# Two more chunks transposed by DMA, a last tile in two halves, and another order of the first slots

## The chip, the cores and the metric

The kernel runs on one NeuronCore of a Trainium2 chip. The metric is the device time of one execution in microseconds (us). The program uses five engines: TensorE (PE in the profile, with its weight loads as PEld), VectorE (DVE), ScalarE (ACT), GpSimd (POOL) and SyncE (SP). Loads that convert float32 to bfloat16 are issued by POOL; stores and DMA transposes are issued by SP. All transfers run on the same 16 DMA engines.

## The reference

The reference has two stages. The first is a retention layer over 4 batches, 8 heads, 768 positions and 64 dimensions per head; the second is a feed-forward layer on its output, with a "snake" activation. Cut to what is computed:

```python
gamma = 1.0 - 2.0 ** (-5.0 - np.arange(H))          # one decay per head
for t in range(S):
    state = gamma[None, :, None, None] * state + np.einsum('bhd,bhe->bhde', k[:, :, t], v[:, :, t])
    y[:, :, t] = scale * np.einsum('bhd,bhde->bhe', q[:, :, t], state)
x = y.transpose(0, 2, 1, 3).reshape(B * S, H * D)   # 3072 tokens x 512
h = x @ w_in                                        # 512 -> 2048
s = np.sin(alpha * h)
g = h + s * s / (alpha + 1e-09)
out = g @ w_out                                     # 2048 -> 512
```

## The kernel before, in words

The positions of a batch are cut into six chunks of 128, so there are 24 chunks. The list `order` (also called `P`) holds them in the order of their processing: first the opening chunk of each of the four batches (P[0] to P[3], named e0 to e3), then the rest of each batch. Counted from one, the seventh and eighth chunks are P[6] and P[7]; below they are called P6, P7 and so on. The chunks form groups of 4, 2, 4, 4, 4, 4 and 2 token tiles (`sizes`), and the feed-forward layer works on one group at a time.

A chunk goes through these steps:

- `load_chunk` (L83) brings q, k and v from HBM into bfloat16 tiles, three transfers issued on POOL's queue. `scale_v` (L112) multiplies v by decay factors, on DVE or POOL.
- q and k must be transposed. `stage_T` (L190 to L200) does it with eight TensorE transposes into a PSUM bank and one copy to the tile qkT on DVE or ACT. `turn` (L202 to L205) does it with one DMA transpose from SBUF to SBUF on SP's queue. The tile qkT has six buffers. Before the change, the chunks up to P7 use TensorE, and P8 and later ones use `turn`.
- `stage_A` (L207 to L218) multiplies k by q for each head (eight matmuls into the PSUM tile pa) and DVE multiplies by a mask (tile aT, L217).
- `stage_M` (L236 to L260) multiplies by v and by the running state, and writes the chunk's columns of xT, the feed-forward layer's input. `stage_S` and `keep_S` (L220 to L234) carry the state.

The feed-forward layer is written as `Slot`s. A Slot is one block of 128 hidden features (or two, with nf=2): four matmuls per block into the PSUM tile ph (L279), a sine on ACT (L282), a square on ACT or DVE (`sq`, L287 or L289), and on DVE the addition that gives gT (`add`, L294). The second matmul of the layer is `ff_out` (L304): 16 matmuls accumulate a 128x512 token tile in the PSUM tile po, then ACT copies it to o_sb (L316) and SP stores it (L317). The very last tile is copied in two halves, by DVE (L313) and then ACT (L314), and stored by one transfer.

PSUM has eight banks, which the program divides as four buffers with the tag mm, two banks with the tag pa, one with ty and one with ps. A buffer is taken again when its last reader has finished.

The order of the work is written out by hand, engine by engine; each engine runs its own list in order and waits for the others by semaphores. The order has these stretches: a start with e0 to e2; "early" Slots 0 to 7 over the first three tiles of group 0, with e3 worked in between; Slots 8 to 15 with the first pieces of `ff_out` for group 0 (helper `F`) and with P4 and P5 worked in; then `phase(1, ...)`, which runs group 1's Slots (nf=2) with the rest of group 0's output. A table in the call of phase 1 says behind which Slot the steps of P6 to P11 stand: T for `stage_T`, X for `turn`, A for `stage_A`, M for `stage_M`. The phases of groups 2 to 6 follow, and the last group's output tiles end the kernel.

Of the kernel before, what the change touches and what calls it, by code (L numbers as in the profile page):

```python
# [8 lines left out]
F32 = mybir.dt.float32  # L9
# [6 lines left out]
def kernel(  # L16
# [15 lines left out]
    nc = tc.nc  # L32
    B, H, S, D = q.shape
    C = 128
# [3 lines left out]
    d_model = H * D  # L38
    d_ff = moe_w_in.shape[1]
    KS = d_model // 128  # L40
    FF = d_ff // 128
# [7 lines left out]
    sizes = [4, 2, 4, 4, 4, 4, 2]  # L49
    assert sum(sizes) == NJ  # L50
    NG = len(sizes)
    groups = [order[sum(sizes[:g]):sum(sizes[:g + 1])] for g in range(NG)]
# [4 lines left out]
    work = ctx.enter_context(tc.tile_pool(name="work", bufs=2))  # L57
    psum = ctx.enter_context(tc.tile_pool(name="psum", bufs=1, space=bass.MemoryType.PSUM))
# [5 lines left out]
    w_out = big.tile([128, FF, d_model], BF16, name="w_out")  # L64
# [4 lines left out]
    def chunk_of(t, j):  # L69
        b, c = divmod(j, NCH)  # L70
        return t[b, :, c * C:(c + 1) * C, :].rearrange("h s d -> s h d")

    def load_chunk(j, names="qkv"):
        for name, src in (("q", q), ("k", k), ("v", v)):
            if name not in names:
                continue
            if name == "v":
                t = big.tile([128, H, D], BF16, name="vr", tag="vr", bufs=NJ)
            else:
                if ("qk", j) not in raw:  # L80
                    raw["qk", j] = big.tile([128, 2, H, D], BF16, name="qkr", tag="qkr", bufs=NJ)
                t = raw["qk", j][:, "qk".index(name)]
            nc.gpsimd.dma_start(out=t, in_=chunk_of(src, j))  # L83
            raw[name, j] = t
# [105 lines left out]
    def stage_T(j, eng=None, tag="ty"):  # L190
        pt = psum.tile([128, 2 * NP, 128], BF16, name="pt", tag=tag, bufs=4 if tag == "mm" else 1)
        st["qkT", j] = work.tile([128, 2 * NP, 128], BF16, name="qkT", tag="qkT", bufs=6)
        for i in range(2):
            for p in range(NP):
                nc.tensor.transpose(pt[:, i * NP + p, :],  # L195
                                    raw["qk"[i], j][:, 2 * p:2 * p + 2, :].rearrange("p h d -> p (h d)"), ident)
        if eng is nc.scalar:
            nc.scalar.copy(st["qkT", j], pt)
        else:
            nc.vector.tensor_copy(st["qkT", j], pt)  # L200

    def turn(j):  # L202

        st["qkT", j] = work.tile([128, 2 * NP, 128], BF16, name="qkT", tag="qkT", bufs=6)
        nc.sync.dma_start_transpose(out=st["qkT", j], in_=raw["qk", j].rearrange("p i h d -> p (i h d)"))  # L205

    def stage_A(j):  # L207
        qkT = st["qkT", j]
        pa = psum.tile([128, 2, NP, 128], F32, name="pa", tag="pa")
        for p in range(NP):  # L210
            for e in range(2):
                r = slice(64 * e, 64 * e + 64)
                nc.tensor.matmul(pa[:, e, p, :], qkT[r, NP + p, :], qkT[r, p, :],  # L213
                                 start=(p == 0), stop=True, skip_group_check=True)
        aT = work.tile([128, 2, NP, 128], BF16, name="aT", tag="aT", bufs=2)
        m = dec.rearrange("p e n t -> p (e n) t") if j % NCH == 0 else mask_bc
        nc.vector.tensor_mul(aT.rearrange("p e n t -> p (e n) t"), pa.rearrange("p e n t -> p (e n) t"), m)  # L217
        st["aT", j] = aT  # L218
# [17 lines left out]
    def stage_M(j):  # L236
        c = j % NCH
        g, i = place[j]
        if g not in xT:
            xT[g] = work.tile([128, KS, sizes[g] * C], BF16, name="xT", tag="xT", bufs=3)  # L240
        qkT, aT, vs = st["qkT", j], st["aT", j], raw["v", j]
        py = psum.tile([128, NP, 128], F32, name="py", tag="ty")
        if c > 0:
            for p in range(NP):
                for e in range(2):
                    r = slice(64 * e, 64 * e + 64)
                    nc.tensor.matmul(py[r, p, :], s_bd[c % 2][:, p, r], qkT[:, p, :],  # L247
                                     start=(p == 0), stop=True, skip_group_check=True)
        for p in range(NP):
            for e in range(2):  # L250
                nc.tensor.matmul(py[64 * e:64 * e + 64, p, :], vs[:, 2 * p + e, :], aT[:, e, p, :],  # L251
                                 start=(c == 0 and p == 0), stop=True, skip_group_check=True)
        x = xT[g][:, :, i * C:(i + 1) * C]
        if c == 0:
            nc.scalar.copy(x, py)
            return
        ps = stage_S(j) if c < NCH - 1 else None
        nc.vector.tensor_mul(x, py, qg[:, c])  # L258
        if ps is not None:
            keep_S(j, ps)  # L260


    gT = {}
# [32 lines left out]

    out_view = out.rearrange("(t p) n -> p t n", p=128)
    po = {}
    end = (NG - 1, sizes[-1] - 1)

    def ff_out(g, ts, f):
        if (g, ts) not in po:
            po[g, ts] = psum.tile([128, d_model], F32, name="po", tag="mm", bufs=4)
        nc.tensor.matmul(po[g, ts], gT[g][:, f, ts * C:(ts + 1) * C], w_out[:, f, :],  # L304
                         start=(f == 0), stop=(f == FF - 1))
        if f == FF - 1:
            take(g, ts)

    def take(g, ts):
        o_sb = work.tile([128, d_model], F32, name="o_sb", tag="o_sb", bufs=3)  # L310
        if (g, ts) == end:
            h = d_model // 2
            nc.vector.tensor_copy(o_sb[:, :h], po[g, ts][:, :h])  # L313
            nc.scalar.copy(o_sb[:, h:], po[g, ts][:, h:])  # L314
        else:
            nc.scalar.copy(o_sb, po[g, ts])  # L316
        nc.sync.dma_start(out=out_view[:, groups[g][ts], :], in_=o_sb)  # L317

    def out_pieces(g, tss):
        return [lambda ts=ts, f=f: ff_out(g, ts, f) for ts in tss for f in range(FF)]  # L320
# [13 lines left out]
    e0, e1, e2, e3 = order[:B]  # L334
# [40 lines left out]
    def phase(g, outs, att, nf=1):  # L375

        no, done = len(outs), 0
        for n in range(FF // nf):
            now = Slot(g, n * nf, nf=nf).sq("A")
            for fn in att.get(n, ()):  # L380
                fn()
            now.add()
            while done < no * (n + 1) * nf // FF:
                outs[done]()
                done += 1

    def T(j):
        return lambda: stage_T(j)

    def X(j):  # L390
        return lambda: turn(j)

    def A(j):
        return lambda: stage_A(j)

    def M(j):
        return lambda: stage_M(j)

    def SK(j):
        return lambda: keep_S(j, stage_S(j))  # L400
# [3 lines left out]
    P = order  # L404
    n3, n4 = 3 * C, 4 * C
    def F(ts, fs):
        for f in fs:
            for t in ts:
                ff_out(0, t, f)

    def early(f, tag="mm"):
        return Slot(0, f, (0, n3), tag=tag)

    a = early(0)
    decay_table(3)
    scale_v(e0, nc.vector)
    for t in s_bd:
        nc.vector.memset(t, 0.0)
    b = early(1)
    a.sq("A").add()  # L420
    a = early(2)
    b.sq("A")
    c = early(3)
    a.sq("A")
    stage_T(e3)
    b.add()
    b = early(4, "ps")
    c.sq("A")
    a.add()
    a = early(5)  # L430
    b.sq("A")
    stage_A(e3)
    c.add()
    c = early(6)
    a.sq("A")
    b.add()
    b = early(7)
    c.sq("A")
# [9 lines left out]
    a = Slot(0, 0, (n3, n4), 4)  # L448
    F((1,), (3,))
    a.sq("A").add()  # L450
    a = Slot(0, 8)
    b = Slot(0, 4, (n3, n4), 4)
    a.sq("A").add()
    a = Slot(0, 9)
    b.sq("D").add()
    F((0, 1), (4,))
    b = Slot(0, 10)
    a.sq("A").add()
    F((0, 1), (5,))
    a = Slot(0, 11)  # L460
# [3 lines left out]
    b = Slot(0, 12)  # L464
# [3 lines left out]
    a = Slot(0, 13)  # L468
    b.sq("D").add()
    F((0, 1), (9,))  # L470
    b = Slot(0, 14)
    a.sq("A").add()
    F((0, 1), (10,))
    stage_T(P[4], nc.scalar, "mm")
    a = Slot(0, 15)
    b.sq("D").add()
    a.sq("A").add()
    F((0, 1), (11, 12))
    stage_A(P[4])
    scale_v(P[4], nc.vector)  # L480
    F((0, 1), (13, 14))
    stage_T(P[5], nc.scalar, "mm")
    F((0, 1), (15,))


    load_chunk(P[7])
    load_chunk(P[8])
    scale_v(P[6], nc.gpsimd)
    load_chunk(P[9])
# [13 lines left out]
    def fill(n):  # L503
        for _ in range(n):
# [9 lines left out]
    stage_M(P[5])  # L514
    fill(4)
    phase(1, outs,
          {0: [T(P[6]), X(P[8])], 1: [A(P[6])], 2: [T(P[7]), X(P[9])], 3: [A(P[7]), M(P[6])], 4: [X(P[10])],
           5: [A(P[8]), M(P[7])], 6: [X(P[11]), A(P[9]), M(P[8]), SK(e1)], 7: [M(P[9])]}, 2)
    for g in range(2, NG):
        att = {}  # L520
        if g + 1 < NG:
            js = groups[g + 1]
            for i, j in enumerate(js):
                a = i * FF // len(js) + 1
                n = P.index(j) + 2
# [6 lines left out]
                    att[a].append(SK(j - 1))  # L532
            att.setdefault(FF - 2, []).append(M(js[-1]))
        phase(g, out_pieces(g - 1, range(sizes[g - 1])), att, 1 if sizes[g] > 2 else 2)
    for fn in out_pieces(NG - 1, range(sizes[-1])):
        fn()
# [1 line left out]
_INS = ['q', 'k', 'v', 'moe_w_in', 'moe_w_out', 'moe_alpha']  # L538
_OUTS = [((3072, 512), 'float32')]
# [25 lines left out]
```

## Time and profile before

The median of nine runs is 219.32 us (218.60 to 220.13). The profiled execution took 220.1 us.

| what | value |
|---|---|
| profiled execution, its own time | 220.1 us |
| its span in the profile | 218.3 us |
| PE busy | 208.0 us (95%) |
| ACT busy | 162.7 us (75%) |
| DVE busy | 128.3 us (59%) |
| POOL busy | 90.0 us (41%) |
| granted TensorE clock | 1.00 |
| DMA transposes (L205), landing after issue | 16, median 5.6 us, 3.1 to 8.6 |
| TensorE transposes of whole chunks (L195) | 40 |
| stores of out tiles, landing after issue | 24, median 2.3 us |

The span runs from the program's first instruction to its last; the time of an execution also holds what lies around it. In the profile a line such as `L279` is a line of the kernel; `out<-in` names the tile written and the tile read. In the timeline a bracket at the end of a row tells how long the engine stood idle before it and what ended that idle time. SPq and POOLq are the instructions with which SP and POOL start transfers.

### The profile page before, as it was taken

Reading aid. Unit: us, or ns where it says so; the run is one execution under the profiler, and the core shown is the slowest. Engines: PE = TensorE matmul, PEld = TensorE weight load, DVE = VectorE, ACT = ScalarE, POOL = GpSimd, SP = SyncE. Lnnn points to the kernel's source line nnn. Section 1 sums busy time; section 2 is a strip of 40 time slices with the busy share of each in tenths; the row PEclk is TensorE's granted clock in tenths of the full one; section 3 lists DMA queues with packets and bytes.
Section 4 is the critical chain, followed back from the end, with each engine's and each line's share of the span. In section 5 each row is a group of like instructions: output and inputs, shape, how many; then the busy total and the mean of one; then the engine's idle time right before and its main releaser. Section 6 shows DMA issues by size and latency. Waiting matters only on the chain.

```text
span 218.3 us, 4245 instructions
## 1 busy us (share of the span) xinstructions
PE 208.0 (95%) x1661; PEld 107.9 (49%) x1661; DVE 128.3 (59%) x213; ACT 162.7 (75%) x311; POOL 90.0 (41%) x105
## 2 busy tenths in 40 slices
PE   7998898999999999999999999999999999999992
PEld 3544553457764544445455445455444544555540
DVE  4686669776896767766466556476464555233310
ACT  7678796558888899798778768768878876766620
POOL 8975333999689797796982000000000000000000
PEclk9999999999999999999999999999999999999999
DMA  9999999999999999999999146136011101111121
GB/s 132 152 192 191 206 207 163 140 196 162 138 146 197 139 162 161 104 147 156 154 193 125 24 96 85 34 77 95 6 50 51 48 0 51 48 48 48 51 92 52
DMA packets 99508, 24.67 MB, mean 113 GB/s; under 512 B 92304, under 2 KB 96416, under 8 KB 99488
## 3 DMA queue, kind: packets, MB, share of 16 engines
q0 software_dynamic: 77024, 13.37, 82.7%
q1 hardware_dynamic: 22464, 11.02, 26.2%
q8 instruction: 13, 0.21, 0.4%
q14 instruction: 7, 0.06, 0.1%
HBM read 27.27 MB, written 6.29 MB: 154 GB/s over the span
## 4 chain that ended last, share of the span: by engine, by line
PE 74%; DMA 12%; POOL 4%; DVE 4%; ACT 2%; issue 1%; POOLq 0%
PE po L304 35%; PE ph L279 30%; DMA qkr<-in_k_dram 8%; DMA w_in<-in_moe_w_in_dram 4%; PE py L247 3%; PE pa L213 2%; POOL qkr L83 2%; PE py L251 2%; DVE aT L217 1%; POOL vr L83 1%; DVE xT L258 1%; PE ps L227 1%; DVE gT L294 1%; PE pt L195 1%; ACT s L282 1%
## 5 line engine op out<-in xcount | busy, mean ns | idle before, releaser
L294 DVE SCALAR_TENSOR_TENSOR gT<-s,rec_alpha,ph 128x512 bf16<-128x512 f32 (+3 forms) x120 | 74.2, 638 | 68.9 <-ACT s L287 68.3
L304 PE MATMUL po<-w_out,gT 128*128 128x512 bf16 x384 | 98.5, 380 | 0.6 <-DVE gT L294 0.6
L279 PE MATMUL ph<-xT,w_in 128*128 128x512 bf16 (+3 forms) x480 | 98.0, 336 | 0.6 <-DVE gT L294 0.2
L282 ACT ACTIVATE s<-ph,alpha_sb 128x512 f32<-128x512 f32 (+3 forms) x120 | 69.7, 602 | 33.7 <-PE ph L279 33.5
L279 PEld LDWEIGHTS <-w_in 128*128 128x128 bf16 x480 | 45.5, 98 | 42.0 <-issue 1.5
L287 ACT ACTIVATE s<-s 128x512 f32<-128x512 f32 (+1 forms) x94 | 58.4, 621 | 2.6
L304 PEld LDWEIGHTS <-gT 128*128 128x128 bf16 x384 | 35.2, 98 | 38.2 <-issue 0.6
L112 POOL TENSOR_TENSOR vr<-vr,kg 128x512 bf16<-128x512 bf16 x21 | 22.1, 1066 | 12.7 <-DMA vr<-in_v_dram 12.7
L217 DVE TENSOR_TENSOR aT<-pa,mask 128x1024 bf16<-128x1024 f32 x20 | 24.4, 1221 | 0.2 <-PE pa L213 0.2
L83 POOL DMA_DIRECT2D vr<-in_v_dram x24 | 21.8, 910 | 3.2 <-DMA w_in<-in_moe_w_in_dram 1.7
L83 POOL DMA_DIRECT2D qkr<-in_q_dram x23 | 21.3, 927 | 3.7 <-DMA w_out<-in_moe_w_out_dram 1.7
L83 POOL DMA_DIRECT2D qkr<-in_k_dram x23 | 20.6, 895 | 5.3 <-DMA w_out<-in_moe_w_out_dram 4.9
L234 ACT CAST s_bd<-ps 64x256 bf16<-64x256 f32 x40 | 14.4, 360 | 2.4 <-PE ps L227 2.1
L316 ACT COPY o_sb<-po 128x512 f32<-128x512 f32 x23 | 13.1, 576 | 3.9 <-PE po L304 3.9
L258 DVE TENSOR_TENSOR xT<-py,qg 128x512 bf16<-128x512 f32 x20 | 13.7, 685 | 2.5 <-PE py L251 2.4
L328 PE MATMUL spare<-warm 128*128 128x512 bf16 x28 | 10.2, 488 | 1.2 <-DVE warm L131 1.2
L213 PEld LDWEIGHTS <-qkT 64*128 64x128 bf16 x192 | 5.4, 94 | 9.3 <-issue 6.9
L251 PE MATMUL py<-aT,vr 128*64 128x128 bf16 x192 | 9.5, 220 | 0.4 <-DVE rec_alpha L366 0.2
L213 PE MATMUL pa<-qkT 64*128 64x128 bf16 x192 | 9.5, 219 | 0.2
L247 PE MATMUL py<-qkT,s_bd 128*64 128x128 bf16 x160 | 8.3, 224 | 0.7 <-DVE xT L258 0.6
L247 PEld LDWEIGHTS <-s_bd 128*64 128x64 bf16 x160 | 5.4, 109 | 4.7 <-issue 2.0
L251 PEld LDWEIGHTS <-vr 128*64 128x64 bf16 x192 | 6.9, 110 | 1.3 <-issue 1.0
(59 smaller groups left out, 69.8 us busy)
## 6 DMA issues: line engine op xcount, KB each, us to landing
out_dram<-o_sb SPq DMA_DIRECT2D x24, 256.0 KB, 2.3
vr<-in_v_dram POOLq DMA_DIRECT2D x24, 128.0 KB, 5.9
qkr<-in_q_dram POOLq DMA_DIRECT2D x23, 128.0 KB, 5.6
qkr<-in_k_dram POOLq DMA_DIRECT2D x23, 128.0 KB, 5.9
w_in<-in_moe_w_in_dram POOLq DMA_DIRECT2D x4, 512.0 KB, 11.1
w_out<-in_moe_w_out_dram POOLq DMA_DIRECT2D x4, 512.0 KB, 14.8
q<-in_q_dram SPq DMA_DIRECT2D x1, 256.0 KB, 3.2
k<-in_k_dram SPq DMA_DIRECT2D x1, 256.0 KB, 4.0
```

Source lines behind the costliest of these rows:

```text
L83: nc.gpsimd.dma_start(out=t, in_=chunk_of(src, j))
L112: eng.tensor_mul(raw["v", j], raw["v", j], kg[:, j % NCH, :, None].to_broadcast([128, H, D]))
L213: nc.tensor.matmul(pa[:, e, p, :], qkT[r, NP + p, :], qkT[r, p, :], start=(p == 0), stop=True, skip_group_check=True)
L217: nc.vector.tensor_mul(aT.rearrange("p e n t -> p (e n) t"), pa.rearrange("p e n t -> p (e n) t"), m)
L247: nc.tensor.matmul(py[r, p, :], s_bd[c % 2][:, p, r], qkT[:, p, :], start=(p == 0), stop=True, skip_group_check=True)
L251: nc.tensor.matmul(py[64 * e:64 * e + 64, p, :], vs[:, 2 * p + e, :], aT[:, e, p, :], start=(c == 0 and p == 0), stop=True, skip_group_che ...
L258: nc.vector.tensor_mul(x, py, qg[:, c])
L279: nc.tensor.matmul(self.ph[:, m, :], w_in[:, i, f * 128:(f + 1) * 128], xT[g][:, i, self.lo:self.hi], start=(m == 0 and i == 0), stop=(i = ...
L282: nc.scalar.activation(out=self.s[:, m, :], in_=self.ph[:, m, :], func=ACTF.Sin, scale=alpha_sb[:, f:f + 1])
L287: nc.scalar.activation(out=self.s, in_=self.s, func=ACTF.Square)
L294: nc.vector.scalar_tensor_tensor(gT[self.g][:, f, self.lo:self.hi], self.s[:, m, :], rec_alpha[:, f:f + 1], self.ph[:, m, :], op0=ALU.mult ...
L304: nc.tensor.matmul(po[g, ts], gT[g][:, f, ts * C:(ts + 1) * C], w_out[:, f, :], start=(f == 0), stop=(f == FF - 1))
```

## The change

There are four edits, all in the order of the work and in where its results are held.

1. `turn` takes the place of `stage_T` for P6 and P7. Both turns stand ahead of phase 1: P6's before the last `F` call of group 0, and P7's right after its load is issued. The table of phase 1 loses its two T entries, and X(P9) moves from Slot 2 to Slot 1. On SP's queue P6's transpose now stands ahead of the first two stores of out tiles, P7's between the second and the third.
2. The last token tile is made in two column halves of 256, each with its own 16 matmuls, copies and store. The first half is copied by ACT, the second by DVE and ACT with 128 columns each.
3. In the early stretch, Slot 1 takes the two pa banks and Slot 4 an mm buffer (it had the ps bank); Slot 1's addition comes earlier; `stage_T(e3)` and `stage_A(e3)` come one Slot later.
4. Around P4, the matmuls of Slot 15 come ahead of `stage_T(P4)`, and Slot 15's square goes from ACT to DVE.

```diff
-    end = (NG - 1, sizes[-1] - 1)
...
         if f == FF - 1:
-            take(g, ts)
-
-    def take(g, ts):
-        o_sb = work.tile([128, d_model], F32, name="o_sb", tag="o_sb", bufs=3)
-        if (g, ts) == end:
-            h = d_model // 2
-            nc.vector.tensor_copy(o_sb[:, :h], po[g, ts][:, :h])
-            nc.scalar.copy(o_sb[:, h:], po[g, ts][:, h:])
-        else:
+            o_sb = work.tile([128, d_model], F32, name="o_sb", tag="o_sb", bufs=3)
             nc.scalar.copy(o_sb, po[g, ts])
-        nc.sync.dma_start(out=out_view[:, groups[g][ts], :], in_=o_sb)
+            nc.sync.dma_start(out=out_view[:, groups[g][ts], :], in_=o_sb)
+
+    def last_tile(g, ts):
+
+        n = d_model // 2
+        for h in range(2):
+            c = slice(h * n, h * n + n)
+            ph = psum.tile([128, n], F32, name="poh", tag="mm", bufs=4)
+            for f in range(FF):
+                nc.tensor.matmul(ph, gT[g][:, f, ts * C:(ts + 1) * C], w_out[:, f, c],
+                                 start=(f == 0), stop=(f == FF - 1))
+            o_sb = work.tile([128, d_model], F32, name="o_sb", tag="o_sb", bufs=3)[:, :n]
+            if h == 0:
+                nc.scalar.copy(o_sb, ph)
+            else:
+                nc.vector.tensor_copy(o_sb[:, :n // 2], ph[:, :n // 2])
+                nc.scalar.copy(o_sb[:, n // 2:], ph[:, n // 2:])
+            nc.sync.dma_start(out=out_view[:, groups[g][ts], c], in_=o_sb)
...
-    b = early(1)
+    b = early(1, "pa")
     a.sq("A").add()
     a = early(2)
-    b.sq("A")
+    b.sq("A").add()
     c = early(3)
     a.sq("A")
+    b = early(4)
+    c.sq("A")
     stage_T(e3)
-    b.add()
-    b = early(4, "ps")
-    c.sq("A")
     a.add()
     a = early(5)
     b.sq("A")
-    stage_A(e3)
     c.add()
     c = early(6)
     a.sq("A")
+    stage_A(e3)
     b.add()
...
     F((0, 1), (10,))
-    stage_T(P[4], nc.scalar, "mm")
     a = Slot(0, 15)
     b.sq("D").add()
-    a.sq("A").add()
+    stage_T(P[4], nc.scalar, "mm")
+    a.sq("D").add()
     F((0, 1), (11, 12))
...
     stage_T(P[5], nc.scalar, "mm")
+    turn(P[6])
     F((0, 1), (15,))
-
-
     load_chunk(P[7])
+    turn(P[7])
+
+
     load_chunk(P[8])
...
-          {0: [T(P[6]), X(P[8])], 1: [A(P[6])], 2: [T(P[7]), X(P[9])], 3: [A(P[7]), M(P[6])], 4: [X(P[10])],
+          {0: [X(P[8])], 1: [A(P[6]), X(P[9])], 3: [A(P[7]), M(P[6])], 4: [X(P[10])],
...
-    for fn in out_pieces(NG - 1, range(sizes[-1])):
+    for fn in out_pieces(NG - 1, range(sizes[-1] - 1)):
         fn()
+    last_tile(NG - 1, sizes[-1] - 1)
```

## The prediction

> **What bounds the kernel now.** I read the page's busy shares first, then the chain of work that ended last, then the timeline from 36 to 66 us, because the chain changes its nature there.
>
> ```profile
> PE 208.0 (95%) x1661; PEld 107.9 (49%) x1661; DVE 128.3 (59%) x213; ACT 162.7 (75%) x311; POOL 90.0 (41%) x105
> ...
> DMA  9999999999999999999999146136011101111121
> ...
> PE 74%; DMA 12%; POOL 4%; DVE 4%; ACT 2%; issue 1%; POOLq 0%
> ```
>
> TensorE sets the end, but 12% of the chain is transfers, and the DMA engines are full for the first 120 us. The chain in order of time shows where that counts:
>
> ```profile
> 20.86 17.95 DMA qkr<-in_k_dram
> 38.86 0.40 PE pt L195 x4
> ...
> 63.79 0.60 DVE xT L258
> 64.38 0.78 DVE gT L294 x2
> 65.17 0.65 DVE xT L258
> 65.86 1.02 PE ph L279 x4
> ```
>
> TensorE cannot pass 38.86 before the k half of chunk P4 lands; the load order sets that moment, not the computation. From 65.86 (first Slot of group 2) TensorE is busy 139.26 of the 139.68 us to 205.54. So whatever moves 65.86 moves the end one for one, and what happens before 38.86 counts only if it uses up the wait there (TensorE idles 0.97 + 0.51 us, for q and for k). Phase 1 lies between, and the timeline shows these rows in it:
>
> ```profile
> 49.85 0.61 PE L195 MATMUL pt<-ident,qkr 128*128 128x128 bf16 x8
> ...
> 50.30 14.28 SPq L205 DMA_TRANSPOSE qkT<-qkr  x4
> ...
> 50.50 0.69 DVE L200 COPY qkT<-pt 128x1024 bf16<-128x1024 bf16 x1 [1.72 <-PE pt L195]
> ...
> 58.99 0.23 PEld L213 LDWEIGHTS <-qkT 64*128 64x128 bf16 x8 [0.28 <-DMA qkT<-qkr]
> ...
> 60.06 1.22 DVE L217 TENSOR_TENSOR aT<-pa,mask 128x1024 bf16<-128x1024 f32 x1
> ```
>
> The first and third rows are P6's transposes on TensorE and their copy on DVE, which the change takes out; the second is what replaces them, four DMA transposes following each other on SP's queue, P8's first. The 58.99 row is the warning: stage_A(P8) already waits 0.28 us for the first DMA transpose, issued at 50.30 and landed 8.6 us later. P9's (53.25) landed 7.2 later at 60.5, its stage_A ran at 61.42: 0.9 us of slack.
>
> **What the Trainium skill says.** "DMA: Bandwidth & Descriptors", section "Queues, rings and completion order": each of the 16 engines goes round robin between the queue rows, and SP's transfers share one row consumed in order. The trace agrees: load packets fall from 9158 in 36 to 44 us (loads alone) to 3887 in 52 to 60, when 2147 packets of SP's queue run. Same page, "Latency and other measured facts": a DMA transpose moves 261 GB/s; the estimate for 256 KB is 1.0 us. The trace does not agree here: landing takes 3.1 us at least, 5.6 median. "TensorE: Matmul & The Clock Gate", "Back-to-back issue gap": 262 cycles for 256 columns, 518 for 512. The trace agrees: 0.87 us for eight of 256, 0.43 for two of 512.
>
> **Part 1, early slots.** The second Slot goes to the pa bank, the fifth to an mm bank, and stage_T(e3) waits behind Slot five. All this ends before 25 us, and TensorE then runs to the fixed 38.86. Worth 0; its cover is the 1.48 us of idle at 38 us. It would cost something only if it lost more than that; the reverse (a gain) only lengthens the wait.
>
> **Part 2, fourth Slot order at P4.** Slot 15's four matmuls (0.86 us, at 39.10) move ahead of stage_T(P4), into the idle time. After 38.86 they are gone. But stage_A(P4) then comes closer to its 1.01 us copy on ACT: before, copy 39.30 to 40.31 and stage_A at 40.91; now it can start near 40.35. F(11,12) fill 0.86 of the interval, so about 0.2 of the 0.86 becomes a wait. Gain 0.65 (bounds 0.4 and 0.86). The square of Slot 15 on DVE, 0.68 us, replaces one of 0.63 on ACT, both idle there.
>
> **Part 3, P6 and P7 by DMA.** Removed: two times eight transposes, 0.44 us each on TensorE (49.85 to 50.30), and two DVE copies of 0.69. TensorE gain 0.88, so stage_A(P6) is due at 51.70 - 0.65 - 0.44 = 50.6, stage_A(P7) at 55.19 - 0.65 - 0.88 = 53.65, stage_A(P8) at 57.2.
>
> Added: two transposes on SP's row. P6's k lands at 43.4 (issue 37.33 + 6.1), so P6's starts at 43.5, ahead of the two out stores of 44.30; with the usual 5.6 to 6.3 us it lands near 49.5: in time. P7's k lands at 45.9; its transpose stands behind both stores in the row and should take like P8's before: 45.9 + 8.6 = 54.5, 0.9 late.
>
> Now what they push. In 36 to 44 us loads alone ran 9158 packets, 1145 per us, so a load of 1024 packets (128 positions times 8 heads) takes 0.89. In 52 to 60, 3887 load packets are 3.4 us of work; the other 4.6 went to two transposes: 2.3 each. (Bounds: 1.0, the page's price, and 3.) In 44 to 52, 6582 load packets are 5.75 us, leaving 2.25 for three stores, 0.75 each. Test: from P7's k (45.9) six loads to P9's k, 5.3, and three stores, 2.25, give 53.5; measured 46.68 + 6.5 = 53.2. So the engines have no room in this stretch, and 4.6 us more come in.
> - P8's k (before 48.5) waits for P6's transpose: 50.8. P8's transpose then stands behind P7's and the third store: 50.8 + 8.6 + about 0.4 = 59.8, before 58.95.
> - P9's k waits for P6's and, shared round robin, about half of P7's: 53.2 + 3.4 = 56.6. Its transpose, with 6.3 (that of P10), lands at 62.9, before 60.5.
>
> What lateness costs: aT(P8) on DVE ran at 60.06 because two gT additions came before it; with TensorE ahead they are done earlier, so P8 may land at 60.06 - 0.45 = 59.6 and cost nothing. After stage_A(P9), M(P8), two out pieces, a Slot and M(P9) take 4.44 us to 65.86, of which 0.34 is a wait for DVE: 4.1. Break-even for P9 is 65.86 - 4.1 = 61.7. P8 is 0.2 over, P9 1.2. Group 2 starts 1.2 us later: all of parts 2 and 3's 1.5 is eaten. Behind the waiting stage_A on TensorE stand all Slots of the phase; ACT and DVE wait for those. Next late would be P10's: its k 4 later at 62.6, transposed at 68.9, due at 68.10 + 1.2 = 69.3: just hidden. The POOL queue keeps its order, but its scale of P9 waits for P9's v, and P11's loads behind it.
>
> **Part 4, last tile.** 32 matmuls of 256 columns for 16 of 512: 3.46 us either way (weight loads of 98 ns fit under 108). The first half's copy and store hide under the second half. Behind the last matmul (214.22) stand now 128x256 on DVE (0.42) then on ACT (0.37), one after the other. From 128x512 and 128x256 (ACT 576 and 372 ns) a 128x128 is about 270, on DVE about 290 by the gT rows (746, 476, 344 ns): saves 0.23. The last store halves: of its 2.0 us landing at most half the 0.75 of work, I take 0.17. Gain 0.4 (bounds 0 and 0.6).
>
> **Sum.** +1.2 - 0.4 = +0.8 on the profiled execution's own 220.1 (span 218.3 and 1.8 around it) gives 220.9; that execution is 0.8 above the median of 219.32, so for a median: 220.1.
>
> **Rivals.**
> B, the transfers are in time (ends on the other side). If the two transposes cost the page's 1.0 us each, P9's k is 1.5 later (54.7) and its transpose lands at 61.0, P8's at about 58.5: group 2 starts up to 1.5 us earlier, with the tail 1.9: 217.4; half of that likelier, 218.0. Speaks for it: quiet transposes land in 3.1, and POOL's three scalings at 52.12 (3.07 us) leave loads unissued. Against: the sum test above and the 8.6. It decides where P9 lands before 61.7 - 0.4.
> C, a wash: lateness just balances the tail, 219.3.
> D, the lateness goes on: P10's and P11's transposes are late too, another 1 to 2 us: 221.8. For: P10's margin of 0.4 us. Against: X(P11) has some 3 us.
> That the change does nothing is excluded: SP's order shows both new transposes.
>
> **How the numbers follow.** Forecast (219.8 to 221.5) 0.44, B (217.2 to 218.9) 0.33, C (218.9 to 219.8) 0.14, D (over 221.5) 0.09. About 0.2%, 0.44 us, is what a measurement of this kernel can tell from no change. Faster: B and a little of C, 0.35; within: the rest of C, 0.12; slower: forecast and D, 0.53. The range leaves out the early end of B (0.10) and the late part of D (0.06): 217.7 to 221.8. Cases of both signs hold most of the chance; the forecast's own range is 219.8 to 221.5.
>
> **What would show it.** Right: TensorE waits at stage_A on qkT's DMA in phase 1, 1 to 3 us in all; P9's k lands after 55; the first matmul of group 2 at 66.5 to 67.5; the end 4 us or less after the last matmul, against 4.08. Part 2: stage_A(P5) 0.6 earlier than 43.84. Wrong: qkT waits under 0.5 us and group 2 before 65.5, because the engines do a transpose in less than 1.5 us beside loads; or a wait at 38 us that outgrew its cover.

## The result

The changed kernel takes 220.73 us (median of 16 executions, 220.04 to 222.23), where the kernel before takes 219.32. The ratio is 1.0074, with a 95% interval of 1.0058 to 1.0090: slower by 1.3 to 2.0 us. A second series gave 220.62 and 1.0061 (1.0035 to 1.0088). The comparisons leave out executions over 1.5% above their kernel's fastest: two in the second series (both 223.05), one of the kernel with P6 alone by DMA (221.43) and four of the kernel before (222.03, 222.29, 222.45 and 423.72).

The profiled execution took 221.69 us, with a span of 219.9. From the page after: the busy shares, the granted TensorE clock and the DMA share in 40 slices of the span, and the chain by engine.

```profile
PE 207.7 (94%) x1661; PEld 109.0 (50%) x1661; DVE 127.7 (58%) x212; ACT 162.6 (74%) x311; POOL 90.0 (41%) x105
...
PEclk9999999999699999999999999999999999999999
DMA  9999999999999999999999946144211101111112
...
PE 76%; DVE 10%; DMA 7%; ACT 5%; issue 2%; SPq 0%; DVEq 0%; ACTq 0%
```

The 16 transposes that TensorE no longer does (0.88 us) hardly show in PE's sum (207.7 us against 208.0), in part because matmuls behind the wait take longer, as the timeline below shows. One slice of the clock line shows 6 instead of 9. The chain after, in order of time (start us, us, what), now passes through a DMA transpose:

```profile
46.15 9.73 DMA qkT<-qkr
...
55.92 0.49 PE pa L213 x8
...
68.13 1.02 PE ph L279 x4
```

It is P7's transpose, 9.73 us from issue to landing, and stage_A(P7) starts as soon as it has landed. Group 2 starts at 68.13, where it started at 65.86. SP's row in the timeline after (start us, us, queue, line, operation) shows how the transfers stand behind each other:

```profile
43.01 1.33 SPq L205 DMA_TRANSPOSE qkT<-qkr  x1
44.38 1.60 SPq L308 DMA_DIRECT2D out_dram<-o_sb  x2
46.15 2.43 SPq L205 DMA_TRANSPOSE qkT<-qkr  x1
48.94 0.34 SPq L308 DMA_DIRECT2D out_dram<-o_sb  x1
49.45 7.29 SPq L205 DMA_TRANSPOSE qkT<-qkr  x2
```

By the landing times, P6's transpose takes from 43.0 to 49.8 us, P7's from 46.15 to 55.9, P8's from 49.45 to 59.4, P9's from 55.2 to 63.0. TensorE's row in the timeline after (the bracket is the idle time before, and what ended it) shows the wait and what follows:

```profile
55.92 0.49 PE L213 MATMUL pa<-qkT 64*128 64x128 bf16 x8 [2.40 <-DMA qkT<-qkr]
56.33 0.64 PE L247 MATMUL py<-qkT,s_bd 128*64 128x128 bf16 x8
...
57.55 1.03 PE L303 MATMUL po<-w_out,gT 128*128 128x512 bf16 x2
58.37 1.60 PE L279 MATMUL ph<-xT,w_in 128*128 128x256 bf16 x8
...
60.24 1.04 PE L279 MATMUL ph<-xT,w_in 128*128 128x256 bf16 x8
```

Two things are here. TensorE waits 2.40 us for P7. After it, eight matmuls of 256 columns take 1.60 us, and two rows later the same eight take 1.04. The windows of core 0 after say why (us, busy time and instructions of PE, PEld, DVE, ACT and POOL, then the granted clock, DMA share, GB/s; the share adds up packets that overlap, so it can pass 1):

```profile
52.92:56.10 3.18, 0.78 (x14) 0.48 (x11) 1.48 (x4) 2.16 (x5) 0.49 (x1) 1.00 1.31 160
56.10:59.50 3.40, 3.40 (x40) 2.28 (x35) 2.60 (x4) 0.73 (x2) 1.38 (x2) 0.50 1.79 155
59.50:61.20 1.70, 1.70 (x14) 1.16 (x12) 0.00 (x0) 1.16 (x3) 1.70 (x3) 1.00 1.98 170
```

For 3.4 us behind the wait, the clock is halved. The balance of the two profiled executions, from one stage_A to the next: to P6 -1.30 us (51.70 to 50.40); P6 to P7 +2.02 (3.49 to 5.51, the wait less the transposes taken out); P7 to P8 +1.49 (3.80 to 5.29, the halved clock); P8 to P9 none (2.43 both); P9 to group 2 +0.06; group 2 to the end of the span -0.67 (152.44 to 151.77), all of it the tail: from the ACT copy of the tile before the last to the end it is 6.87 us (from 213.03) instead of 7.54 (from 210.76). The sum is +1.60, which is 219.9 less 218.3. The tail in the timeline after:

```profile
214.78 0.37 ACT L321 COPY o_sb<-poh 128x256 f32<-128x256 f32 x1 [1.16 <-PE poh L317]
...
216.58 0.29 DVE L323 COPY o_sb<-poh 128x128 f32<-128x128 f32 x1 [6.32 <-PE poh L317]
216.91 0.27 ACT L324 COPY o_sb<-poh 128x128 f32<-128x128 f32 x1 [1.75 <-DVE o_sb L323]
```

The end comes 3.3 us after the DVE copy's start, where it was 4.08 after the last matmul.

The halved clock is not in every execution. One halved stretch of 3.4 us in 218 makes a mean clock of 0.992. Of the 16 executions six have that mean, and take 221.63 us on average; the other ten have 0.998 to 1.0, and take 220.42. In the second series it was 5 of 13, the two of 223.05 among them.

### The profile page after: what moved, and what is told of

Read it like the earlier page. It is cut to its first block, busy times and chain, and to the rows that moved or that the text cites. A ratio compares the mean times of both kernels' runs of the same rounds, so it can differ in the third digit from the quotient of the medians.

```text
span 219.9 us, 4253 instructions
## 1 busy us (share of the span) xinstructions
PE 207.7 (94%) x1661; PEld 109.0 (50%) x1661; DVE 127.7 (58%) x212; ACT 162.6 (74%) x311; POOL 90.0 (41%) x105
## 3 DMA queue, kind: packets, MB, share of 16 engines
q1 hardware_dynamic: 24720, 11.55, 28.4%
## 4 chain that ended last, share of the span: by engine, by line
PE 76%; DVE 10%; DMA 7%; ACT 5%; issue 2%; SPq 0%; DVEq 0%; ACTq 0%
PE po L303 32%; PE ph L279 31%; DMA qkT<-qkr 4%; DVE gT L294 3%; PE pa L213 3%; DVE aT L217 3%; PE py L247 2%; DMA k<-in_k_dram 2%; PE py L251 2%; ACT s L282 2%; PE poh L317 2%; DVE xT L258 1%; PE ps L227 1%; PE spare L336 1%; ACT qkT L198 1%
## 5 line engine op out<-in xcount | busy, mean ns | idle before, releaser
L303 PE MATMUL po<-w_out,gT 128*128 128x512 bf16 x368 | 95.5, 381 | 0.0
L287 ACT ACTIVATE s<-s 128x512 f32<-128x512 f32 (+1 forms) x93 | 57.7, 621 | 2.6
L303 PEld LDWEIGHTS <-gT 128*128 128x128 bf16 x368 | 33.6, 98 | 35.6
L336 PE MATMUL spare<-warm 128*128 128x512 bf16 x28 | 9.4, 458 | 1.2 <-DVE warm L131 1.2
```

The costliest lines, as they stand in the source:

```text
L287: nc.scalar.activation(out=self.s, in_=self.s, func=ACTF.Square)
```

## Experiments

The leading theory: the DMA engines have no room in 44 to 60 us, so every transpose added there makes itself and the transfers behind it late (R, for room). The rivals: P7's place in SP's row, behind two stores, makes it late (S); the halved clock makes most of the loss (H); one of the other edits costs time (O). Each ratio is to the kernel before, with its 95% interval.

**The change without its two DMA transposes.** P6 and P7 are transposed by TensorE again; the other three edits stay.

```diff
     stage_T(P[5], nc.scalar, "mm")
-    turn(P[6])
     F((0, 1), (15,))
     load_chunk(P[7])
-    turn(P[7])
...
-          {0: [X(P[8])], 1: [A(P[6]), X(P[9])], 3: [A(P[7]), M(P[6])], 4: [X(P[10])],
+          {0: [T(P[6]), X(P[8])], 1: [A(P[6])], 2: [T(P[7]), X(P[9])], 3: [A(P[7]), M(P[6])], 4: [X(P[10])],
```

> The changed kernel with P6 and P7 transposed on TensorE again, as before the change; the three other edits stay. My theory (the late DMA transpose of P7 in phase 1, and the TensorE clock that falls to 0.68 behind its wait, cost everything): no wait on qkT's DMA for P7, group 2 starts about 0.7 us earlier than in the kernel before, and with the shorter tail the time is about 218.0, a ratio of 0.993 to 0.996. Rival (the early slots' order or P4's order loses the time): it stays near 220.5.

Measured: 218.49 us, 0.9960 (0.9945 to 0.9976). No matmul of stage_A waits for qkT's DMA. P8's transpose, issued at 49.40 as in the changed kernel, lands at 57.8 instead of 59.4, and group 2 starts at 64.95. None of 22 executions has a mean clock below 0.997. So the whole loss, and more, hangs on the two transposes, and O falls. This version is 2.2 us faster than the changed kernel and 0.9 faster than the one before.

**Only the two transposes, in the kernel before.** The reverse edit:

```diff
     stage_T(P[5], nc.scalar, "mm")
+    turn(P[6])
     F((0, 1), (15,))
     load_chunk(P[7])
+    turn(P[7])
...
-          {0: [T(P[6]), X(P[8])], 1: [A(P[6])], 2: [T(P[7]), X(P[9])], 3: [A(P[7]), M(P[6])], 4: [X(P[10])],
+          {0: [X(P[8])], 1: [A(P[6]), X(P[9])], 3: [A(P[7]), M(P[6])], 4: [X(P[10])],
```

> The kernel before with the two DMA transposes alone, no other edit. My theory: stage_A(P7) is due 0.7 us later than in the changed kernel, so the wait is near 1.7 instead of 2.4 us, but the landing near 56 us sets group 2 all the same, the clock falls too, and there is no shorter tail: 221.3 to 221.8, a ratio near 1.010. Rival (another edit loses the time): within 0.2% of the kernel before.

Measured: 221.39 us, 1.0075 (1.0043 to 1.0108). In 4 of 8 executions the mean clock is 0.992 (221.62 us on average, the others 220.60). From the waits of this kernel (engine, what waited and for what: us in all, times, the longest):

```profile
PE pa L213 <- DMA qkT<-qkr: 3.2, 2, 2.2
```

The two waits stand at P7 (stage_A at 56.85) and P9 (64.02), and group 2 starts at 67.87. The transposes alone bring the loss: about 1.1 us without the halved clock (220.60 less 219.48, the median of the kernel before in that series), from only four executions, which lie between 219.66 and 221.96.

**P7's transpose ahead of the stores.** In the changed kernel, P7's load and turn go ahead of the last `F` of group 0, so that on SP's row both new transposes stand ahead of all three stores. POOL's order stays.

```diff
     turn(P[6])
-    F((0, 1), (15,))
     load_chunk(P[7])
     turn(P[7])
+    F((0, 1), (15,))
```

> The changed kernel with P7's load and DMA transpose moved ahead of the last output pieces of group 0's first two tiles, so that on SP's queue P7's transpose stands ahead of the first two stores instead of behind them; POOL's order stays. If the place behind the stores in SP's row makes P7 late: it lands near 52.5 instead of 55.9, the wait is under 0.5 us, the clock holds, and the time is 217.7 to 218.5. Rival (the DMA engines have no room, whatever the order): it lands after 55, the wait is 2 us or more, the time stays at 220.5 or goes up.

Measured: 220.18 us, 1.0052 (1.0025 to 1.0079). P7's transpose lands at 53.6, 2.3 us earlier. TensorE's weight loads in the timeline of this kernel (P7, P8, P9):

```profile
53.68 0.23 PEld L213 LDWEIGHTS <-qkT 64*128 64x128 bf16 x8 [0.44 <-DMA qkT<-qkr]
...
59.10 0.23 PEld L213 LDWEIGHTS <-qkT 64*128 64x128 bf16 x8 [1.89 <-DMA qkT<-qkr]
...
62.34 0.23 PEld L213 LDWEIGHTS <-qkT 64*128 64x128 bf16 x8 [1.02 <-DMA qkT<-qkr]
```

Neither theory had all of this. The place in the row moves P7's own landing, as S says; but the wait only goes on to P8 and P9, as R says, and the ratio is lower by 0.2% only, with overlapping intervals. Three of the 14 executions have a mean clock of 0.992 or less, so the move did not end the fall.

**Filling the wait.** Ten matmuls on constant data, whose result nobody reads, stand on TensorE ahead of stage_A(P7). They do nothing for the transfers.

```diff
+    def fill_pe(n):
+        t = psum.tile([128, 512], F32, name="keep", tag="ty")
+        for _ in range(n):
+            nc.tensor.matmul(t, warm[:, :128], warm, start=True, stop=True)
...
-          {0: [X(P[8])], 1: [A(P[6]), X(P[9])], 3: [A(P[7]), M(P[6])], 4: [X(P[10])],
+          {0: [X(P[8])], 1: [A(P[6]), X(P[9])], 3: [lambda: fill_pe(10), A(P[7]), M(P[6])], 4: [X(P[10])],
```

> The changed kernel with ten matmuls of 512 columns on constant data (some 2.2 us, results unused) put ahead of stage_A(P7), where TensorE waits 2.4 us. If the wait alone costs the time: the same as the changed kernel, 220.5 to 221. If the fall of the granted clock behind the wait costs another 1.5 us: the clock stays at 1.00 in the stretch behind stage_A(P7), stage_A(P8) follows 3.8 us after it instead of 5.3, and the time is 219.0 to 219.5.

Measured: 220.09 us, 1.0043 (1.0023 to 1.0062), between the two times expected. The fill's row in TensorE's timeline, and the windows' row behind it (columns as above):

```profile
54.05 2.32 PE L417 MATMUL keep<-warm 128*128 128x512 bf16 x10
```

```profile
56.30:60.88 4.58, 3.66 (x53) 2.75 (x54) 3.10 (x6) 2.73 (x7) 0.02 (x1) 1.00 2.25 142
```

The work takes the place of nearly all of the wait at P7 (smaller waits come at P8 and P9 in this profile, 1.1 us in all), and the clock stays whole: none of 22 executions has a mean below 0.997. The mean time, 220.39, is that of the changed kernel's executions without the fall, 220.42. So the halved clock here comes from TensorE's idleness, and is worth 0.45 us on average (six of 16 times 1.2). H holds for that part, and for no more: 1.0043 is still slower than before. Five of the 22 take 221.16 to 222.02 us at a whole clock, the profiled one among them; the clock is not all that scatters, and what makes these five slow is not shown.

**Two transposes nobody reads.** Into the first experiment's kernel, where TensorE transposes P6 and P7, come two DMA transposes of the same data at the places they have in the changed kernel, to tiles that nobody reads any more. No step waits for them; they only load the engines and SP's row.

```diff
+    def dummy_turn(j):
+        t = near["q" if j == P[6] else "k"].bitcast(BF16).rearrange("p h (a d) -> p (h a) d", a=1)
+        nc.sync.dma_start_transpose(out=t, in_=raw["qk", j].rearrange("p i h d -> p (i h d)"))
...
     stage_T(P[5], nc.scalar, "mm")
+    dummy_turn(P[6])
     F((0, 1), (15,))
     load_chunk(P[7])
+    dummy_turn(P[7])
```

> P6 and P7 on TensorE, and at the two places on SP's queue the same two DMA transposes all the same, into tiles that nobody reads any more. What changes against the variant with both on TensorE (ratio 0.996) is only the DMA engines' load. If the engines have no room: P8's transpose lands 1.5 to 3 us later than 57.8, stage_A(P8), due at 58.0, waits 1.5 to 2.5 us, P9's lands past 62, and the time is 219.8 to 221. If only the lateness of P7's own transpose cost: P8 lands before 58.5 and the ratio stays within 0.002 of 0.996.

Measured: 221.29 us, 1.0098 (1.0067 to 1.0130), 2.8 us over the same kernel without them. P6 and P7 are in time (50.28 and 53.77). TensorE's weight loads in the timeline of this kernel, P8's and P9's:

```profile
59.41 0.23 PEld L213 LDWEIGHTS <-qkT 64*128 64x128 bf16 x8 [2.12 <-DMA qkT<-qkr]
...
63.47 0.23 PEld L213 LDWEIGHTS <-qkT 64*128 64x128 bf16 x8 [1.83 <-DMA qkT<-qkr]
```

P8's transpose lands 10.1 us after its issue, at 59.4, to a tenth where the changed kernel has it. The transfers alone, with no step waiting for their results, cost the time, somewhat more than R's forecast of 219.8 to 221: this is R. The unread transposes load the engines and also stand ahead of P8's in SP's row, and the run does not part these two. But loads on POOL's queue are late too: in 44 to 52 us their k halves land 10.4 us after issue, where it was 6.7 without the unread transposes. So the engines' share counts; what the row adds stays open. The clock is 1.0 in all five executions, though both waits are near 2 us.

**One of the two.** Two kernels: P6 by DMA and P7 on TensorE, and P7 by DMA (behind the two stores, as in the change) and P6 on TensorE. With P6 alone, X(P9) goes back to Slot 2; the order on SP's row stays. All else as changed.

```diff
     load_chunk(P[7])
-    turn(P[7])
...
-          {0: [X(P[8])], 1: [A(P[6]), X(P[9])], 3: [A(P[7]), M(P[6])], 4: [X(P[10])],
+          {0: [X(P[8])], 1: [A(P[6])], 2: [T(P[7]), X(P[9])], 3: [A(P[7]), M(P[6])], 4: [X(P[10])],
```

> The changed kernel with P7 on TensorE again and P6 still by DMA. If each DMA transpose costs because it takes DMA engine time from the loads and transposes behind it: P6's own lands in time near 50, but P8's lands at 58.5 to 59.5 against a due time near 57.6, a wait of about 1 us, and the time is 218.7 to 219.5, worse than with both on TensorE (ratio 0.996). If only the lateness of P7's own transpose cost: no wait, TensorE saves 0.44 us more than with both on TensorE, and the ratio is 0.993 to 0.995.

```diff
     stage_T(P[5], nc.scalar, "mm")
-    turn(P[6])
     F((0, 1), (15,))
...
-          {0: [X(P[8])], 1: [A(P[6]), X(P[9])], 3: [A(P[7]), M(P[6])], 4: [X(P[10])],
+          {0: [T(P[6]), X(P[8])], 1: [A(P[6]), X(P[9])], 3: [A(P[7]), M(P[6])], 4: [X(P[10])],
```

> The changed kernel with P6 on TensorE again and P7 by DMA, its transpose behind two stores on SP's queue as in the changed kernel. If the number of added transposes decides: about the same as with P6 alone by DMA, a ratio of 0.996 to 0.998, with P7's landing before 54. If the place behind the stores decides: P7 still lands after 54.5, stage_A(P7) waits over 0.5 us, and the ratio is over 0.999.

Measured: P6 alone 218.43 us, 0.9969 (0.9949 to 0.9989); P7 alone 219.00, 0.9989 (0.9971 to 1.0006). Neither is better than none by DMA (0.9960). With P6 alone, its transpose lands at 49.7, P8's at 56.6 in time, and P9's stage_A waits 1.06 us, at 60.34. Neither forecast for it came: R had P8 late and 218.7 us or more, its rival no wait at all and a ratio of 0.995 or less. The waits with P7 alone (P7 and P8 in the timeline of weight loads):

```profile
53.43 0.23 PEld L213 LDWEIGHTS <-qkT 64*128 64x128 bf16 x8 [0.51 <-DMA qkT<-qkr]
57.71 0.23 PEld L213 LDWEIGHTS <-qkT 64*128 64x128 bf16 x8 [0.76 <-DMA qkT<-qkr]
```

P7 lands at 53.4 behind the two stores (R's forecast was before 54, with a ratio up to 0.998): 2.5 us earlier than with P6's transpose beside it. (The stores, too, start 1.7 us earlier than in the changed kernel, at 42.68, as no transpose stands ahead of them.) With both transposes ahead of the stores it landed at 53.6. So P7 is late only when P6's transpose and the stores are both ahead of it. S falls as the main cause of the loss, since with the stores behind the two transposes the ratio is still 1.0052. Against the kernel with none, one transpose costs 0.1 to 0.3% (0.1 is within the noise) and two cost 1.1%: one still nearly finds room, two don't.

**The other edits, one at a time, in the kernel before.** The tail in two column halves:

```diff
-    end = (NG - 1, sizes[-1] - 1)
...
+    def last_tile(g, ts):
...
-    for fn in out_pieces(NG - 1, range(sizes[-1])):
+    for fn in out_pieces(NG - 1, range(sizes[-1] - 1)):
         fn()
+    last_tile(NG - 1, sizes[-1] - 1)
```

> The kernel before with the last tile in two column halves alone. My sum: from the last matmul to the end 3.7 us instead of 4.1, the 32 half-width matmuls take the same 3.46 us as the 16, and the time falls by 0.4 us, a ratio of 0.998; the profile of the changed kernel makes 0.6 to 0.75 likelier, 0.997. Rival (twice as many weight loads slow the matmuls): the half-width matmuls take 3.7 us or more and the gain is gone.

Measured: 219.00 us, 0.9985 (0.9972 to 0.9999), so a gain of 0.33 us. The copies behind the last matmul in its timeline are the two of the changed kernel, 0.29 and 0.27 us, and its span ends 3.5 us after the first of them starts. The half-width matmuls are not quite free: from the ACT copy of the tile before to that first copy it is 3.55 us (210.26 to 213.81, and the same in the changed kernel), where it was 3.46 (210.76 to 214.22).

The order at P4:

```diff
-    stage_T(P[4], nc.scalar, "mm")
     a = Slot(0, 15)
     b.sq("D").add()
-    a.sq("A").add()
+    stage_T(P[4], nc.scalar, "mm")
+    a.sq("D").add()
```

> The kernel before with the matmuls of Slot 15 ahead of P4's transposes, and Slot 15's square on DVE, alone. My sum: stage_A(P5) 0.65 us earlier against the landing of P4's k than before, all carried to the end: a ratio of 0.997. Rival (the early slots make the gain, P4's order nothing, since the transfers of phase 1 set the pace): within 0.1% of before.

Measured: 219.31 us, 0.9994 (0.9977 to 1.0010): nothing. The early slots' order alone:

```diff
-    b = early(1)
+    b = early(1, "pa")
     a.sq("A").add()
     a = early(2)
-    b.sq("A")
+    b.sq("A").add()
     c = early(3)
     a.sq("A")
-    stage_T(e3)
-    b.add()
-    b = early(4, "ps")
+    b = early(4)
     c.sq("A")
+    stage_T(e3)
...
-    stage_A(e3)
     c.add()
     c = early(6)
     a.sq("A")
+    stage_A(e3)
```

> The kernel before with the other order and banks of the early slots alone. My prediction's step: worth nothing, since TensorE then waits for P4's load at 38 us: within 0.1% of before. Rival (in most executions P4's load is in time, as in the profiles of the later runs, where it landed near 37.5 instead of 38.8, and the wait for e3's q and k near 18 us, 0.9 us in the profile before, is carried to the end): a ratio of 0.996 to 0.998.

Measured: 219.33 us, 1.0007 (0.9991 to 1.0022). Both together:

> The kernel before with the early slots' order and P4's order together, neither tail nor turns. Each alone measured a ratio of 1.0007 and 0.9994. If they add up: 0.999 to 1.001, and the variant with both transposed on TensorE (0.996) owes its gain to the tail (0.9985) and to the scatter of the measurement. If each hides the other's gain (the wait for e3's load and the wait at P4 in turn): 0.996 to 0.998.

Measured (the two diffs above in one kernel): 219.27 us, 1.0001 (0.9980 to 1.0021). The two orders bring nothing, alone or together. What the first experiment has (0.9960) beyond the tail's 0.9985 stays unsettled: the intervals meet, and scatter may be all of it.

Why P4's order brings nothing shows in the time from stage_A(e3) to stage_A(P4), the first and second row of each fence. The kernel before took 19.88 us (21.03 to 40.91) in its profiled execution. The tail alone, which has the same code in this stretch, and then P4's order alone:

```profile
21.39 0.23 PEld L213 LDWEIGHTS <-qkT 64*128 64x128 bf16 x8 [0.32 <-issue]
...
40.41 0.23 PEld L213 LDWEIGHTS <-qkT 64*128 64x128 bf16 x8 [0.42 <-ACT s L282]
```

```profile
20.27 0.23 PEld L213 LDWEIGHTS <-qkT 64*128 64x128 bf16 x8 [0.32 <-issue]
...
39.17 0.22 PEld L213 LDWEIGHTS <-qkT 64*128 64x128 bf16 x8 [0.73 <-ACT qkT L198]
```

That is 19.02 and 18.90 us. The kernel before waits for P4's load in its own profile, and the same code takes 0.86 less in the next; the kernel with the transposes alone takes 19.02 too (22.13 to 41.15). With the early order, where stage_A(e3) comes later, it is 18.32 us, and 18.21 with P4's order added. So where the load is in time, P4's order is worth 0.1 us. The reason is another wait, from TensorE's timeline with the tail alone and then with P4's order alone:

```profile
38.60 1.02 PE L279 MATMUL ph<-xT,w_in 128*128 128x512 bf16 x4 [0.62 <-DVE gT L294]
```

```profile
37.47 0.61 PE L195 MATMUL pt<-ident,qkr 128*128 128x128 bf16 x8 [0.38 <-DVE gT L294]
...
39.18 0.40 PE L213 MATMUL pa<-qkT 64*128 64x128 bf16 x8 [0.24 <-ACT qkT L198]
```

In the old order Slot 15's matmuls wait 0.62 us for a PSUM buffer of the tag mm, until DVE's addition has read it. In the new order the transposes of P4 come second and wait for such a buffer instead, 0.38 us, and stage_A(P4) then waits 0.24 us for the copy: 0.62 again.

**The changed kernel again,** for a profile without the fall of the clock.

> The changed kernel itself once more, for the granted clock. If its fall to 0.992 of the span's mean follows from the wait at stage_A(P7) by chance, some of the executions show it and some don't, and those that do are 1 to 1.5 us longer; the others stand near 220.4. If the fall in the first profile was an accident of that execution alone, no execution shows it and all stand near 220.4.

Measured: 220.62 us, 1.0061 (1.0035 to 1.0088). Its profiled execution has mean clock 0.999. Its waits, and the window from stage_A(P7) to stage_A(P8):

```profile
PE pa L213 <- DMA qkT<-qkr: 2.9, 2, 2.0
```

```profile
56.53:60.27 3.74, 3.74 (x53) 2.76 (x54) 2.60 (x4) 1.90 (x5) 0.00 (x0) 1.00 1.84 156
```

The same stretch takes 3.74 us instead of 5.29, so the fall cost 1.55 us there. P9, due earlier now, waits 1.11 us, but part of that is slack: from stage_A(P7) to group 2 (67.45) it is 10.92 us instead of 12.22, so the fall cost 1.3 in the end, near the 1.2 that the averages show.

## Why the prediction was right, and where it was not

**The whole.** 220.1 was predicted, 217.7 to 221.8; 220.73 was measured. Slower was the likelier side, at 0.53 not by much, and its mechanism, transposes and loads that make each other late in phase 1, is the one that the runs show. The sizes inside it are less good than the total, as follows.

**Part 3, P6 and P7 by DMA: right in kind, P7 mis-sized, P8 and P9 right by luck.** The landings predicted for P6, P8 and P9 were 49.5, 59.8 and 62.9; the first profile has 49.8, 59.4 and 63.0. For P8 and P9 two errors cancel. P8's k was not held up (47.5, predicted 50.8), so its transpose was issued at 49.45, but took 9.9 us instead of 9.0. P9's k landed at 55.1 (predicted 56.6, though "after 55" holds), and its transpose took 7.8 us instead of 6.3. The loads were less late than priced, and the transposes slower. P7 was put at 54.5, by the 8.6 us that P8's took before, and landed at 55.9, 9.73 after its issue. So the wait comes first at P7, and 2.4 us instead of 0.9. The step that failed is this term: the 8.6 were taken over unchanged, though P6's transpose is now in flight ahead of P7's. The kernel without P6's lands P7's at 53.4, 7.5 after its issue; with the stores behind it, it took 8.1.

What was counted as group 2's lateness, +1.2, is about +1.1 by the kernel with the transposes alone, in its executions without the fall, and +1.4 by the changed kernel's (220.42, with the tail's 0.33 put back, less 219.32). Group 2 was to start at 67.06 (66.5 to 67.5). The first profile's 68.13 lies outside, by the fall of the clock, which the forecast did not have; the second profile has 67.45. Once P9 is late, only 3.86 us pass from its stage_A to group 2 in that profile, not the 4.1 of the sum.

The claim that the engines have no room rested on 2.3 us of engine time for each transpose. The DMA view after, in 52 to 60 us (queue: packets, MB, share):

```profile
DMA  9999991117999999999999999999999999999999
...
q0 software_dynamic: 3780, 0.48, 98.6%
q1 hardware_dynamic: 2172, 0.77, 72.4%
```

Over 44 to 60 us, 8515 load packets at the prediction's 1145 per us are 7.4 us of work, three stores 2.25; 6.3 are left for 3216 packets of transposes. SP's queue carries 24,720 packets in all with both transposes and 23,664 with one of the two, so one transpose is 1056 packets. By this estimate 3.0 transposes took 6.3 us, 2.1 each. It is an upper one, since what is left also holds the stretches in which the engines stood nearly idle; so were the prediction's 2.3. Rival B's price, an estimate of 1.0 us from the rate that the Trainium skill gives ("DMA: Bandwidth & Descriptors", section "Latency and other measured facts"), does not fit the waits seen here.

**The missed term: the clock.** Nothing in the prediction speaks of it. The Trainium skill, "TensorE: Matmul & The Clock Gate", "Part 1: The HAM clock gate", says that the clock halves after an idle window of about 3.4 us, and that this window runs free of what the kernel does; the section "HAM oscillation" warns of idle gaps over 3.4 us. The halved stretch agrees (3.4 us at 0.50). The gap does not: 2.40 us of wait were enough here, in some executions. In the 3.18 us before the fall TensorE was busy for 0.78, so it was not wholly idle either. That the window's phase decides which execution falls would fit, but no run shows the phase. The term is 0.45 us on average, most of the 0.6 that the forecast is short of.

**Part 2, P4's order: wrong.** A gain of 0.65 was predicted, none was measured. The failed step is "the load order sets that moment": the 1.48 us of idle time at 38 us were a property of the one profiled execution, as the other profiles show. The sign that was named, stage_A(P5) 0.6 us earlier than 43.84, came in one profile of the changed kernel (42.98) and not in the other (43.96). In a profile of the same code the stretch is 0.86 us shorter; what waits there is 0.62 us for a PSUM buffer, and the new order only spreads that wait over two places (0.38 and 0.24). The sum did not suffer, since the gain was booked as eaten by the late transfers.

**Part 1, early slots: right** (0 predicted, 1.0007 measured), though the cover that was named for it was that same idle time.

**Part 4, the tail: right.** 0.4 predicted, 0.33 measured, with copies of 0.29 and 0.27 us as predicted (290 and 270 ns), and the end 3.3 us after the last copies begin ("4 us or less"). The step "3.46 us either way" was 0.09 short.

**The rivals.** B, in time, is excluded by the waits and by the two transposes that nobody reads. C, a wash, and D, lateness that goes on to P10, did not come either: from 68.13 to 207.50 us TensorE is busy 138.95 of 139.37.

## What to carry to other kernels

Before work goes from an engine to DMA, count what the DMA engines already carry in that stretch, packet by packet, and look at the next transfers in the row: here a saving of 0.88 us of TensorE time made the kernel 2.2 us slower, in part by waits at chunks that the change doesn't touch. A wait seen in one profiled execution is not yet cover to hide an edit in; look for it in a second profile of the same code. And a new wait of some 2 us on TensorE can cost more than its length, so price the clock too.

## What was unexpected in the hardware

- The granted clock fell to half for 3.4 us behind a wait of 2.4 us, in 6 of 16 executions and 5 of 13 of the same kernel, in 4 of 8 with the transposes alone, in 3 of 14 with P7's transpose ahead of the stores, and in 1 of 12 with P6 alone by DMA. It did not in the five executions of the kernel with the unread transposes, whose profile has waits of 2.12 and 1.83 us. Such a mean clock is not bound to late transposes alone: the kernel before has one execution at or under 0.992 of the 50 beside the second series (222.03 us), and P4's order alone one of 22 (219.87); neither was profiled. Ten filling matmuls ended it (none of 22). Where the limit lies stays open.
- A 256 KB transpose from SBUF to SBUF beside loads lands 9.7 us after its issue with one ahead of it and one behind (P7's in the changed kernel), in 7.5 with only the one behind (P7 alone, 45.85 to 53.4); 3.1 is the least in the whole kernel.
- The DMA line above has a hole from 53.2 to 53.8 us, engines at a tenth, while P7's and P8's transposes are under way. The added transposes are not its cause: the kernel before has such a hole from 62.8 to 63.7 us, and the kernel with none of the two from 61.8 to 62.5. So "no room" is not the whole of it: transposes can be outstanding while the engines stand nearly idle. No run here shows what holds them up.
- The landing of a load early in the kernel varies between executions by enough to make 0.9 us of TensorE's wait come and go: the wait for P4's load at 38 us is in the first profile of the kernel before and not in the next profile of the same code.
